# Weight residuals on VectorE alone, and the short chunk's value products in two column halves, in a fused attention, expert and MLP kernel

## The chip, the cores and the metric

The kernel runs on one core of a Trainium2 chip. The metric is the device time of one execution in microseconds (us), the median of several runs. A core has the engines TensorE (PE; its weight loads are shown apart as PEld), VectorE (DVE), ScalarE (ACT), GpSimd (POOL) and SyncE (SP), which issues most of the DMAs. Every engine works through its own instructions in order, and semaphores tie them together.

## The reference

Three parts run one after another. Each takes the output of the part ahead of it.

```python
# attention: 2 batches, 8 heads, 576 tokens, head size 64, with a position bias per head
scores = scale * q @ k.T + bias[h, i, j]
attn = exp(scores - max) / sum;  x = attn @ v              # -> 1152 tokens x 512
# experts: 8 of them, 512 -> 1024 -> 512, one expert per token, up to 288 tokens each
e = argmax(x @ w_gate);  y = gate * (relu(x @ w1[e]) @ w2[e])   # 0 for tokens over the capacity
# MLP: 512 -> 2048 -> 512
h = y @ w_in;  out = max(0.01 * h, h) @ w_out
```

## The kernel before, in words

**Attention.** The 576 query rows of a batch are four chunks of 128 rows and a short chunk of 64. `order` lists the ten (batch, chunk) pairs; each has four units, one per pair of heads, so there are 40 units, n = 0 to 39. The short chunks are units 16 to 19 (first batch) and 36 to 39 (second batch, the last of all). The loop at the end of the function is a software pipeline written out by hand. In turn n, PE makes the scores of unit n+1 (`s0`, `qk`, tile `St`, L329), transposes the weights of unit n (`tr`, tile `pt`, L362 to L368) and multiplies those of unit n-1 by V (`pv`, tile `xp`, L399 for full chunks, L402 and L404 for short ones). DVE adds the bias and takes the maximum (`ttr`, L341); ACT makes the exponential (`expo`, tile `A`, L352) and copies the transposed weights (L372). `prep`, `hooks`, `fin_a`, `fin_b` and `fin_c` hang routing, loads and clean-up on given turns. In a short chunk two heads share one unit: rows 0 to 63 of the score tile are head 2p, rows 64 to 127 are head 2p+1. `pv` of such a unit multiplies all 128 columns of V of both heads by all 128 rows and `fin_a` (L412) reads only the two 64x64 blocks on the diagonal.

**Residuals.** Matrices of the expert and MLP stages are used as a pair of float32r numbers, high part and residual, and each product is three matmuls (high times high, high times low, low times high; L856 to L858, L1191 to L1193). `wsplit` makes the pair for a weight tile of 128x1024: ACT casts it into `P[:, 0]` (L671), and an engine given by the caller writes the difference into `P[:, 1]` (L672).

**Experts.** `big_step` does one of eight steps of a block of up to 288 tokens: it splits the weights that are two steps ahead, then does two groups of the up (steps 0 to 3) or down product. The first block's first two splits stand in `hooks` at turns 36 and 37; the block itself follows the attention, then a second block (`big_last`) and a block of up to 64 tokens (`small`).

**MLP.** `chunk` takes 608 tokens through 16 weight tiles in the order `PO`: four up steps, four down steps, four up, four down. An up step has four half groups (`up_half`): PE multiplies 12 times into one of three PSUM tiles `g` (L856 to L858); ACT makes 0.01 times it (L880); DVE takes the maximum (L881, which frees the PSUM tile); a group later `split_h` makes the pair (ACT L888, DVE L889, tile `hq`). Between the groups `next(cv)` puts one of the three DVE operations (`conv_op`, L685, L687, L689) that turn the 64-bit weight words of `w_in` and `w_out` into floats, tile `raw`. Step i first calls `wsplit` for the tile of step i+2; in an up step that tile is the one whose third `conv_op` ran in the step before. The down steps (`down_tok`) use PE alone, besides `wsplit` and `conv_op`.

Of the kernel before, what the change touches and what calls it, by code (L numbers as in the profile page):

```python
# [26 lines left out]
NFULL = S // 128  # L27
# [47 lines left out]
def tile_attention_moe_mlp(ctx, tc, qc, kc, vc, wpk, cst, ctok, cap, wm, wo, out):  # L75
    nc = tc.nc
# [56 lines left out]
    def setup_late():  # L133
        nc.sync.dma_start(tok, ctok)
        nc.sync.dma_start(cpi, cap.to_broadcast([128, 2]))
        nc.gpsimd.memset(acc, 0.0)
        nc.gpsimd.memset(oh, 0.0)
        nc.gpsimd.memset(kcum, 0.0)
        nc.gpsimd.memset(pat, 0.0)
        nc.gpsimd.memset(pat[:, :, 0:1].bitcast(I32), OOB)  # L140
        nc.gpsimd.tensor_tensor(out=II, in0=ident[:, 0:CAPS], in1=ident[:, CAPS : 2 * CAPS], op=ALU.add)

        nc.gpsimd.memset(pre, 0.0)
        nc.gpsimd.memset(pre[:, DM : DM + 1].bitcast(I32), OOB)
# [3 lines left out]
    def prefill(t, a, n):  # L148
        w = t.shape[1]
        nc.sync.dma_start(t.rearrange("(a p) c -> p a c", p=128)[:, a : a + n], pre[:, 0:w].unsqueeze(1).to_broadcast([128, n, w]))  # L150
# [60 lines left out]
    def flush(n):  # L211
        g = drip.pop(n)
        while g in dq:
            run(dq.pop(0))

    def queue(n, g):
        drip[n] = g
        dq.append(g)
# [172 lines left out]
    def pv(c, p, ATs, Vs, xp):  # L391
        V, vt, vd = Vs
        AT, AX_ = ATs
        if c < NFULL:
            for t in range(NFULL + 1):
                for j in range(2):
                    h = 2 * p + j
                    w, a = (V[:, t, 64 * h : 64 * h + 64], AT[:, j, 128 * t : 128 * t + 128]) if t < NFULL else (vd[:, p, 64 * j : 64 * j + 64], AX_)
                    nc.tensor.matmul(xp[64 * j : 64 * j + 64, p, :], w, a, start=t == 0, stop=t == NFULL)  # L399
        else:  # L400
            for t in range(NFULL):
                nc.tensor.matmul(xp[:, p, :], V[:, t, 128 * p : 128 * p + 128], AT[:, 0, 128 * t : 128 * t + 128],  # L402
                                 start=t == 0, stop=False)
            nc.tensor.matmul(xp[:, p, :], vt[:, 128 * p : 128 * p + 128], AX_[0:64], start=False, stop=True)  # L404

    def fin_a(c, rs, xp, last):
        xt = rt.tile([128, NP, 128], F32, name="xt", tag="xt", bufs=1)
# [256 lines left out]
    raws, Ps, xhls, regs = [], [], [], {}  # L664
# [5 lines left out]
    def wsplit(raw, P_, eng):  # L670
        nc.scalar.copy(P_[:, 0], raw)  # L671
        eng.tensor_tensor(out=P_[:, 1], in0=raw, in1=P_[:, 0].bitcast(F32), op=ALU.subtract)  # L672
# [87 lines left out]
    def hooks(n):  # L760
        if n == 1:
            setup_late()
        if n == 12:
            nc.vector.tensor_copy(capf, cpi[:, 0:1])
        if n in PF:
            prefill(srt, 3 * PF.index(n), 3)
        if n == 16:
            nc.sync.dma_start(sid.rearrange("(p a) c -> p a c", p=128), pat)
        if n == NB0 + 4:
            queue("acc0", route_acc(0, range(NCH)))  # L770
        if n == NB0 + 5:
            flush("acc0")
            queue("route0", route0())
            queue("first0", first0())
        if n == SC[0]:
            flush("route0")
        if n in SC:
            scatter(0, SC.index(n))
        if n in ACC1:
            queue("acc1", route_acc(1, [i for i in range(NFULL) if ACCN[i] == n]))  # L780
        if n - 1 in ACC1:
            flush("acc1")
        if n == RF + 1:
            flush("first0")
            regs["e0"] = nc.values_load(ints[0:1, 2:3], engines=[SP], min_val=0, max_val=E_N - 1)
            regs["x0"] = nc.values_load(ints[0:1, 3:4], engines=[SP], min_val=0, max_val=S)
        if n in (CV0 - 3, CV0 - 2, CV0 - 1):
            g_w64(n - CV0 + 3)
        k, odd = divmod(n - CV0 - 2, 2)
        if odd == 0 and 0 <= k < len(CVA):  # L790
            nc.sync.dma_start(wsc[CVA[k]], cvd[k])
            if k + 3 < len(CVA):
                g_w64(k + 3)
        if n == 36:
            for t, m in xtiles:
                if t % 2 == 0:
                    kr = p1.tile([128, 2, S], F32, name="x0r", tag="kr", bufs=KRB)
                x0.append(kr[:, t % 2, 0:DM])
                nc.sync.dma_start(x0[t][0:m], srt[sl_(regs["x0"] + 128 * t, m), 0:DM])
            copy_id(regs["x0"], 0, CAPB)  # L800
        if n in (33, 34, 36, 37):
            raws.append(wp.tile([128, 1024], F32, name="raw", tag="bs", bufs=5))
            wdma(wsrc(regs["e0"], len(raws) - 1), raws[-1])
        if n in (36, 37):
            Ps.append(wp.tile([128, 2, 1024], F32R, name="P", tag="G", bufs=3))
            wsplit(raws[n - 36], Ps[-1], nc.gpsimd)
        if n == 38:
            xhls.append(wp.tile([128, 2, NP, CAPB], F32R, name="xhl0", tag="G", bufs=3))
        if n in (38, 39):
            wdma(wsrc(regs["e0"], n - 34), raws[n - 38])  # L810
        if n >= 38:
            x_tr(n - 38, x0[n - 38], xhls[0])
        if n == N:
            route1a()
            scatter(1, 0)
            scatter(1, 1)

    def tail_part(fa):
        att.close()
        mo = ctx.enter_context(tc.tile_pool(name="mo", bufs=1))  # L820
        spare = wp.tile([128, 1024], F32, name="spare", tag="bs", bufs=5)
# [226 lines left out]
        def big_step(j, base, eng, post=None, prep=False, last=None):  # L1048
            split((j + 2) % 8, eng, R0 if post else R8)
            if j == 7:  # L1050
                down_last(Ps[3], F1 // 128, CAPB, lambda m: (yout(base, m), last and last(m)))
            for mm in range(2):
                if j < 4:
                    up_group(Ps[j], j, mm, xhls[0], CAPB)
                elif j < 7:
                    down_group(Ps[j - 4], j - 4, mm, F1 // 128, CAPB)
                if post:
                    post(j, mm)
            if prep and j >= 5:
                prep_x(j - 5)  # L1060

        def big_last():
            xbase, base = bval(0, 1, 1, [SP]), bval(0, 1, 2, [ACT, DVE, SP])
            copy_id(xbase, base, CAPB)
            ne = bval(1, 0, 0, [SP])
            for j in range(8):
                big_step(j, base, nc.gpsimd)
                if j > 2:
                    wdma(wsrc(ne, j - 3), R8[j - 3])

# [133 lines left out]
        def chunk(c, first):  # L1204
            w = MCS[c]
            groups = [(t, min(128, w - 128 * t)) for t in range(-(-w // 128))]
            cv = convs()
            PP = [Ds[i] if first and i < 2 else Ps[i % 4] for i in range(16)]
            if not first:
                for i in range(3):  # L1210
                    wdma(wsc[i], raws[i])
                yprep(c)
            for i in range(3, 5):
                conv_start(i)
            if not first:
                for i in range(2):
                    wsplit(raws[i], PP[i], nc.vector)
            for i in range(13):
                if i + 2 < 16:
                    wsplit(spare if first and i == 0 else raws[(i + 2) % 4], PP[i + 2], nc.gpsimd)  # L1220
                q = PO[i]
                if q < 8:
                    for g in (0, 2, 1, 3):
                        up_half(PP[i], 2 * q + g // 2, w // 2 * (g % 2), w // 2)
                        if g != 3:
                            next(cv, None)
                else:
                    for kk in range(2):
                        for t, n in groups:
                            down_tok(PP[i], 2 * (q - 8) + kk, t, n)  # L1230
                            if t == 0:
                                split_h()
                            if 2 * t + kk in DCV:
                                next(cv, None)
                if i == 5:
                    for t, n in groups:
                        nc.sync.dma_start(idg[0:n, t], sid[MOF[c] + 128 * t : MOF[c] + 128 * t + n].bitcast(I32))
            wsplit(raws[15 % 4], PP[15], nc.vector)
            for t, n in groups:
                for i in range(13, 16):  # L1240
                    for kk in range(2):
                        down_tok(PP[i], 2 * (PO[i] - 8) + kk, t, n)
                emit(t, n)
# [21 lines left out]
    for n in range(N + 1):  # L1265
# [9 lines left out]
        if n + 1 < N:  # L1275
            b, c, p = units[n + 1]
# [12 lines left out]
        if n >= 1:  # L1289
            b, c, p = units[n - 1]  # L1290
# [74 lines left out]
```

## Time and profile before

| | |
|---|---|
| median of 3 runs | 407.12 us (406.49 to 407.96) |
| the profiled execution | 408.05 us, of which its span, first to last instruction, is 406.3 us |
| busy, share of the span | PE 93%, PEld 77%, DVE 76%, ACT 60%, POOL 34% |
| granted TensorE clock, mean | 0.986 of full speed |
| DMA | 81.79 MB, mean 201 GB/s |

Matmuls overlap in the pipeline, so a busy PE need not be one at its peak; where PE lost time shows in the distance from start to start. A row of the timeline gives the start, the duration and, in brackets, the idle time before it and what ended that.

### The profile page before, as it was taken

Reading aid. Unit: us, or ns where it says so; the run is one execution under the profiler, and the core shown is the slowest. Engines: PE = TensorE matmul, PEld = TensorE weight load, DVE = VectorE, ACT = ScalarE, POOL = GpSimd, SP = SyncE. Lnnn points to the kernel's source line nnn. Section 1 sums busy time; section 2 is a strip of 40 time slices with the busy share of each in tenths; the row PEclk is TensorE's granted clock in tenths of the full one; section 3 lists DMA queues with packets and bytes.
Section 4 is the critical chain, followed back from the end, with each engine's and each line's share of the span. In section 5 each row is a group of like instructions: output and inputs, shape, how many; then the busy total and the mean of one; then the engine's idle time right before and its main releaser. Section 6 shows DMA issues by size and latency. Waiting matters only on the chain. (4 is left out here: it accounts for less than half of the span.)

```text
span 406.3 us, 8427 instructions
## 1 busy us (share of the span) xinstructions
PE 375.9 (93%) x2990; PEld 312.6 (77%) x2990; DVE 307.7 (76%) x733; ACT 242.9 (60%) x522; POOL 139.1 (34%) x110
## 2 busy tenths in 40 slices
PE   4777999988999999999999999999999999899993
PEld 2234666756688888988889999998988778788872
DVE  5998989899854888899458972137899999999310
ACT  3857898788865878767654875556544222455100
POOL 1445857574101110212332206840242255222311
PEclk9999899999999999999998999999999999999997
DMA  7979599798879938889185299683243366530011
GB/s 180 320 235 322 157 330 313 274 297 250 216 236 262 353 135 233 224 253 250 46 236 201 69 327 343 217 289 114 106 173 127 106 207 206 209 106 2 19 59 51
DMA packets 34050, 81.79 MB, mean 201 GB/s; under 512 B 8427, under 2 KB 8811, under 8 KB 31952
## 3 DMA queue, kind: packets, MB, share of 16 engines
q1 hardware_dynamic: 32880, 78.70, 61.3%
q0 software_dynamic: 1120, 2.48, 1.7%
q8 instruction: 25, 0.41, 0.4%
q14 instruction: 25, 0.20, 0.2%
HBM read 59.11 MB, written 23.20 MB: 203 GB/s over the span
## 5 line engine op out<-in xcount | busy, mean ns | idle before, releaser
L341 DVE CUSTOM_DVE_ANT_0 sv<-St,bt 128x576 f32<-128x576 f32 x72 | 52.9, 750 | 30.8 <-PE St L329 18.8
L672 POOL TENSOR_TENSOR P<-raw,P 128x1024 fp32r<-128x1024 f32 x18 | 45.3, 2521 | 76.6 <-ACT P L671 63.5
L352 ACT ACTIVATE A<-sv,mx 128x576 f32<-128x576 f32 x72 | 59.3, 837 | 3.2 <-DVE mx L341 3.0
L329 PE MATMUL St<-K,Q 128*128 128x320 f32 (+1 forms) x320 | 53.6, 310 | 2.6 <-DVE mx L341 2.2
L329 PEld LDWEIGHTS St<-K,Q 128*128 128x128 f32 x320 | 43.9, 189 | 14.6 <-issue 8.4
L182 PE MATMUL pb<-Gt,WP 128*32 128x272 f32 (+17 forms) x352 | 42.1, 505 | 13.3 <-DVE Gt L165 7.5
L269 POOL TENSOR_TENSOR Q<-qr,Q 128x256 fp32r<-128x256 f32 x22 | 16.9, 769 | 99.9 <-ACT Q L261 62.1
L165 DVE TENSOR_SCALAR Gt<-WL,bp 128x400 f32<-128x400 f32 (+17 forms) x98 | 49.4, 563 | 0.1
L671 ACT CAST P<-raw 128x1024 fp32r<-128x1024 f32 x27 | 28.3, 1048 | 28.3 <-DVE raw L689 22.7
L362 PE MATMUL pt<-CS,A 128*128 128x128 f32 x288 | 41.5, 284 | 1.3 <-ACT A L352 0.8
L372 ACT COPY AT<-pt 128x512 f32<-128x512 f32 x40 | 23.3, 583 | 29.2 <-PE pt L362 28.9
L362 PEld LDWEIGHTS pt<-CS,A 128*128 128x128 f32 x288 | 38.1, 206 | 2.2 <-ACT A L352 1.3
L169 POOL TENSOR_SCALAR Gt<-WL,bp 128x528 f32<-128x528 f32 (+12 forms) x17 | 34.1, 2009 | 8.2 <-DVE Gt L165 7.3
L399 PE MATMUL xp<-AT,V 128*64 128x128 f32 x512 | 35.9, 284 | 0.0
L399 PEld LDWEIGHTS xp<-AT,V 128*64 128x64 f32 x512 | 28.0, 139 | 9.8 <-issue 9.5
L182 PEld LDWEIGHTS pb<-Gt,WP 128*32 128x32 f32 x352 | 12.4, 110 | 29.8 <-DVE Gt L165 14.7
L856 PE MATMUL g<-yhl,P 128*128 128x304 f32 x96 | 30.5, 318 | 3.9 <-DVE gfa L881 3.9
L193 ACT ACTIVATE bs<-pb,CS 128x288 f32<-128x288 f32 (+53 forms) x60 | 27.2, 500 | 10.1 <-PE pb L182 9.5
L1193 PE MATMUL ac<-P,hq 128*128 128x512 f32 (+1 forms) x80 | 31.5, 394 | 0.0
L1191 PE MATMUL ac<-P,hq 128*128 128x512 f32 (+1 forms) x80 | 31.5, 394 | 0.0
L1192 PE MATMUL ac<-P,hq 128*128 128x512 f32 (+1 forms) x80 | 31.5, 394 | 0.0
L889 DVE TENSOR_TENSOR hq<-gfa,hq 128x304 fp32r<-128x304 f32 x32 | 28.9, 902 | 1.4 <-ACT hq L888 1.4
(322 smaller groups left out, 907.4 us busy)
## 6 DMA issues: line engine op xcount, KB each, us to landing
bt<-scr SPq DMA_DIRECT2D x24, 576.0 KB, 6.0
w<-wo SPq DMA_DIRECT2D x13, 1024.0 KB, 5.0
scr<-bs SPq DMA_DIRECT2D x36, 295.5 KB, 4.2
raw<-wm SPq DMA_DIRECT2D x14, 512.0 KB, 6.2
w<-wm SPq DMA_DIRECT2D x10, 512.0 KB, 5.7
srt<-pre SPq DMA_DIRECT2D x6, 771.0 KB, 8.4
qr<-qc SPq DMA_DIRECT2D x16, 256.0 KB, 5.7
w64g<-wo SPq DMA_DIRECT2D x3, 1024.0 KB, 10.3
```

The costliest lines, as they stand in the source:

```text
L165: nc.vector.tensor_scalar(G, src, bp[:, g : g + 1], 0.0, op0=ALU.add, op1=ALU.max)
L169: nc.gpsimd.tensor_scalar(G, src, bp[:, g : g + 1], 0.0, op0=ALU.add, op1=ALU.max)
L182: nc.tensor.matmul(pb[32 * q : 32 * q + 32, 0 : hi - lo], W2, gs[:, q, lo:hi], start=True, stop=True)
L329: nc.tensor.matmul(St[:, o + lo : o + hi], Q[:, h - 2 * p, w, :], K[:, h - 2 * p, lo:hi], start=n == 0, stop=n == len(seq) - 1)
L341: nc.vector.tensor_tensor_reduce(out=sv, in0=St, in1=bt[:, jb], scale=-0.125, scalar=3.0e38, op0=ALU.add, op1=ALU.min, accum_out=mx)
L352: nc.scalar.activation(A[:, :, j], sv, AF.Exp, bias=mx, scale=-1.0, accum_out=rs[:, col : col + 1])
L362: nc.tensor.transpose(pt[:, 128 * t : 128 * t + 128], A[:, 128 * t : 128 * t + 128, j], ident)
L399: nc.tensor.matmul(xp[64 * j : 64 * j + 64, p, :], w, a, start=t == 0, stop=t == NFULL)
L672: eng.tensor_tensor(out=P_[:, 1], in0=raw, in1=P_[:, 0].bitcast(F32), op=ALU.subtract)
L1191: nc.tensor.matmul(ps, hh, wh, start=k == 0, stop=False)
L1192: nc.tensor.matmul(ps, hh, wl, start=False, stop=False)
L1193: nc.tensor.matmul(ps, hl, wh, start=False, stop=k == F2 // 128 - 1)
```

## The change

Three calls that gave `nc.gpsimd` to a weight split give `nc.vector`: the two in `hooks`, the eight of `big_last`, and the 13 in the loop of `chunk`. The loop `any_block`, which doesn't run with these inputs, keeps GpSimd. In `pv`, a short unit's five matmuls (128 columns of V by 128 rows) become ten, each head's 64 columns by its own 64 rows; the two halves of the output sit in different column halves of PE's array, as they do in full chunks.

```diff
@@ pv
-            for t in range(NFULL):
-                nc.tensor.matmul(xp[:, p, :], V[:, t, 128 * p : 128 * p + 128], AT[:, 0, 128 * t : 128 * t + 128],
-                                 start=t == 0, stop=False)
-            nc.tensor.matmul(xp[:, p, :], vt[:, 128 * p : 128 * p + 128], AX_[0:64], start=False, stop=True)
+            for t in range(NFULL + 1):
+                for j in range(2):
+                    r = slice(64 * j, 64 * j + 64)
+                    h = slice(128 * p + 64 * j, 128 * p + 64 * j + 64)
+                    w, a = (V[:, t, h], AT[:, 0, 128 * t + 64 * j : 128 * t + 64 * j + 64]) if t < NFULL else (vt[:, h], AX_[0:64, r])
+                    nc.tensor.matmul(xp[r, p, r], w, a, start=t == 0, stop=t == NFULL)
@@ hooks
-            wsplit(raws[n - 36], Ps[-1], nc.gpsimd)
+            wsplit(raws[n - 36], Ps[-1], nc.vector)
@@ big_last
-                big_step(j, base, nc.gpsimd)
+                big_step(j, base, nc.vector)
@@ chunk
-                    wsplit(spare if first and i == 0 else raws[(i + 2) % 4], PP[i + 2], nc.gpsimd)
+                    wsplit(spare if first and i == 0 else raws[(i + 2) % 4], PP[i + 2], nc.vector)
```

Line numbers behind `pv` are two higher in the changed kernel. In its order of instructions, DVE around the `hooks` of turns 36 and 37 (L341 is `ttr`, of units 38 and 39 here; the row with `mx` alone reads its minimum out) had before:

```order
L415 TENSOR_SCALAR rs<-rs 128x8
L341 ISA sv,mx<-St,bt 128x576
L341 ISA mx 128x1
L417 RECIPROCAL rec<-rs 128x8
L439 TENSOR_TENSOR xn<-px,rec 128x512
L341 ISA sv,mx<-St,bt 128x576
L341 ISA mx 128x1
```

and has now, with L674 the residual:

```order
L417 TENSOR_SCALAR rs<-rs 128x8
L674 TENSOR_TENSOR P<-raw,P 128x1024
L341 ISA sv,mx<-St,bt 128x576
L341 ISA mx 128x1
L419 RECIPROCAL rec<-rs 128x8
L441 TENSOR_TENSOR xn<-px,rec 128x512
L674 TENSOR_TENSOR P<-raw,P 128x1024
L341 ISA sv,mx<-St,bt 128x576
```

A residual stands ahead of each of the two `ttr`, so these wait behind it.

In the MLP, DVE around the end of one up step and the start of the next (`gfa` is the half group's float result) had before:

```order
L689 SCALAR_TENSOR_TENSOR raw<-w_3172,raw 128x1024
L881 TENSOR_TENSOR gfa<-g_3189,gfa 128x304
L889 TENSOR_TENSOR hq_3175<-gfa,hq_3173 128x304
L881 TENSOR_TENSOR gfa<-g_3190,gfa 128x304
L889 TENSOR_TENSOR hq_3175<-gfa,hq_3173 128x304
L685 TENSOR_SCALAR raw<-w_3171 128x1024
```

and has now:

```order
L691 SCALAR_TENSOR_TENSOR raw<-w_3212,raw 128x1024
L883 TENSOR_TENSOR gfa<-g_3229,gfa 128x304
L891 TENSOR_TENSOR hq_3215<-gfa,hq_3213 128x304
L674 TENSOR_TENSOR P_3210<-raw,P_3210 128x1024
L883 TENSOR_TENSOR gfa<-g_3230,gfa 128x304
L891 TENSOR_TENSOR hq_3215<-gfa,hq_3213 128x304
L687 TENSOR_SCALAR raw<-w_3211 128x1024
```

The residual came in ahead of the new step's first L881 (now L883); nothing else moved.

On PE, a short unit's products (turn 37) stood before between the transposes and those of the routed rows, `pxs`:

```order
L362 MATMUL pt<-CS,A 128x128 x4
L368 MATMUL pt_3049<-CS,A 64x128
L402 MATMUL xp<-AT,V 128x128 x4
L404 MATMUL xp<-AX__3001,vt 128x128
L723 MATMUL pxs<-CS,x0r 128x128 x4
```

and stand there now as:

```order
L362 MATMUL pt<-CS,A 128x128 x4
L368 MATMUL pt_3074<-CS,A 64x128
L406 MATMUL xp<-AT,V 64x64 x8
L406 MATMUL xp<-AX__3021,vt 64x64 x2
L725 MATMUL pxs<-CS,x0r 128x128 x4
```

Twice as many matmuls of a quarter of the output each; their place is the same.

## Rows read from the trace of the kernel before

**Rows 1.** Timeline of PE (start us, us): a stall, and where the second up stage begins and ends.
```profile
306.18 0.41 PE L856 MATMUL g<-yhl,P 128*128 128x304 f32 x1 [0.94 <-DVE gfa L881]
...
341.20 0.30 PE L856 MATMUL g<-yhl,P 128*128 128x304 f32 x1
...
346.08 0.30 PE L858 MATMUL g<-yhl,P 128*128 128x304 f32 x1
...
371.65 0.39 PE L1191 MATMUL ac<-P,hq 128*128 128x512 f32 x1
```

**Rows 2.** Timeline of DVE, third and fourth up step: start us, us, engine, line.
```profile
303.08 2.06 DVE L889 TENSOR_TENSOR hq<-gfa,hq 128x304 fp32r<-128x304 f32 x1
...
306.05 0.46 DVE L889 TENSOR_TENSOR hq<-gfa,hq 128x304 fp32r<-128x304 f32 x1
...
308.33 1.21 DVE L689 SCALAR_TENSOR_TENSOR raw<-w,raw 128x1024 uint32<-128x1024 uint32 x1
...
311.04 0.47 DVE L881 TENSOR_TENSOR gfa<-g,gfa 128x304 f32<-128x304 f32 x1 [0.73 <-ACT gfa L880]
```

**Rows 3.** Timeline of POOL, an up step and a down step.
```profile
302.41 2.40 POOL L672 TENSOR_TENSOR P<-raw,P 128x1024 fp32r<-128x1024 f32 x1 [5.95 <-ACT P L671]
...
326.19 2.91 POOL L672 TENSOR_TENSOR P<-raw,P 128x1024 fp32r<-128x1024 f32 x1 [4.68 <-ACT P L671]
```

**Rows 4.** Timeline of ACT, the cast ahead of the fourth up step's residual.
```profile
309.63 1.05 ACT L671 CAST P<-raw 128x1024 fp32r<-128x1024 f32 x1 [1.13 <-DVE raw L689]
```

**Rows 5.** Timeline of DVE, down steps and the second up stage's first L881.
```profile
326.87 3.31 DVE L689 SCALAR_TENSOR_TENSOR raw<-w,raw 128x1024 uint32<-128x1024 uint32 x1
...
346.41 0.47 DVE L881 TENSOR_TENSOR gfa<-g,gfa 128x304 f32<-128x304 f32 x1
```

**Rows 6.** Groups by line, DVE: x, busy us, mean ns of one, idle before.
```profile
L672 DVE TENSOR_TENSOR P<-raw,P 128x1024 fp32r<-128x1024 f32 x9 | 10.9, 1219 | 3.0 <-ACT P L671 1.8 <-DMA out<-pre 1.2
```

**Rows 7.** Page, part 6: DMA issues, KB each, median us to landing.
```profile
w<-wo SPq DMA_DIRECT2D x13, 1024.0 KB, 5.0
```

**Rows 8.** Timeline of PE, turn 37: products of a short unit (x: passes).
```profile
202.02 0.43 PE L444 MATMUL pl<-xt,WP 128*32 128x128 f32 x8
202.38 1.16 PE L402 MATMUL xp<-AT,V 128*128 128x128 f32 x8
203.47 0.48 PE L404 MATMUL xp<-AX__2949,vt 64*128 64x128 f32 x2
203.88 1.34 PE L329 MATMUL St<-K,Q 128*128 128x320 f32 x8
```

**Rows 9.** Timeline of PE: products of a full unit, two column halves.
```profile
198.50 1.09 PE L399 MATMUL xp<-AT,V 128*64 128x128 f32 x16
...
199.74 1.34 PE L329 MATMUL St<-K,Q 128*128 128x320 f32 x8
```

**Rows 10.** Timeline of PE: the same operation as L444 above, 64 columns wide.
```profile
214.08 0.33 PE L444 MATMUL pl<-xt,WP 128*32 128x64 f32 x8
214.33 0.61 PE L856 MATMUL g<-xhl,P 128*128 128x288 f32 x1
```

**Rows 11.** Timeline of ACT, turns 36 to 38.
```profile
200.73 1.05 ACT L671 CAST P<-raw 128x1024 fp32r<-128x1024 f32 x1
...
206.42 0.82 ACT L352 ACTIVATE A<-sv,mx 128x576 f32<-128x576 f32 x1
```

**Rows 12.** Timeline of DVE: `ttr` of unit 38.
```profile
201.11 0.76 DVE L341 CUSTOM_DVE_ANT_0 sv<-St,bt 128x576 f32<-128x576 f32 x1 [1.99 <-PE St L329]
```

**Rows 13.** Timeline of PE, turns 38 and 39; L453 is `fin_c`'s.
```profile
205.05 0.63 PE L362 MATMUL pt<-CS,A 128*128 128x128 f32 x4
...
207.53 0.64 PE L362 MATMUL pt<-CS,A 128*128 128x128 f32 x4
...
209.51 0.33 PE L453 MATMUL pl<-CS,lt 128*128 128x128 f32 x1
```

**Rows 14.** Windows: us, busy of PE, PEld, DVE, ACT, POOL, PEclk, DMA share, GB/s.
```profile
214.40:217.40 3.00, 3.00 (x14) 2.93 (x14) 2.81 (x13) 1.26 (x2) 1.02 (x1) 0.50 0.92 352
```

## The prediction

> **What bounds the kernel now.** I read the windows first, then PE's starts in the timeline, then the other engines around PE's gaps. By starts, PE is packed through both short chunks; the exceptions that matter are the MLP's up stages and the end of the attention.
>
> In an up step PE stalls about 1 us for L881, which frees a PSUM tile [rows 1]. The second up stage runs from 341.20 to 371.65, 30.45 us. Its matmuls start (346.08 - 341.20) / 35 = 0.139 us apart where nothing stalls, so its 4 x 48 need 26.8 us: 3.65 us are lost there. DVE sets this pace, and what stretches DVE is to be seen by laying two timelines over each other. One L889 of a step takes 2.06 us, the others 0.46 [rows 2]. The long one began at 303.08, in the middle of POOL's residual, 302.41 to 304.81 [rows 3], and ended 0.33 after it: it ran when POOL was done. L881, which reads PSUM, isn't held: the one at 311.04 took 0.47 [rows 2], though its step's residual had begun when the cast ended at 310.68 [rows 4]. In the down steps L689 is held in this way: 3.31 us from 326.87, over a residual from 326.19 to 329.10 [rows 3, 5], against 1.21 [rows 2]. So DVE's high busy share is partly waiting for POOL.
>
> **Up steps, removed and added.** Gone: 2.06 - 0.46 = 1.60 us of DVE for a held L889. Added: the residual on DVE, 1.22 us [rows 6], of which 0.08 overlap the next operation, so 1.14. But in order it must wait for ACT's cast, and the cast for the third conversion, L689. From the start of that L689: 1.21 to its end [rows 2], 0.09 to the cast (308.33 + 1.21 = 309.54; 309.63), 1.05 for the cast [rows 4], 0.06 handover, 1.14: the next step's first L881 starts 3.55 us after L689. Now it starts 2.71 after (308.33 to 311.04), so 0.84 are added there. A cycle thus changes by +0.84 - 1.60 = -0.76 us, from 8.35 (311.04 less 302.69, since L881 starts 0.39 ahead of the L889 at 303.08) to 7.6. PE's own need is 48 x 0.139 = 6.7, so PE still waits and the gain passes through. The first up stage has two such full cycles between its stalls: **-1.5**.
>
> **Down steps.** PE isn't waiting here, but DVE falls behind: the second up stage's first L881 runs at 346.41 [rows 5], though PE began the stage at 341.20 and its first group was ready for L881 some 2.4 us later (12 x 0.139, then 0.3 of pipeline and an ACT operation of 0.42). Four L689 are held by 2.1 each, 8.4 together; four residuals of 1.14 cost 4.6. DVE gets there 3.8 us sooner against PE, at 342.6 in the old time, before PE has the group. In the four up steps DVE then needs 4 x (8 x 0.39 + 0.61 + 3 x 1.14) = 28.6 us, plus up to 0.4 per cast, against PE's 26.8; but PE may run three PSUM tiles ahead, 3 x 1.67 us, which covers the difference. I take back 3.5 of the 3.65: **-3.5**. From 371.65 on PE runs without a wait, so what is gained there reaches the end.
>
> What can spoil it: the conversions read 1 MB of words per tile, 5.0 us from issue to landing [rows 7], asked for when the conversion two tiles back is done. Two cycles of 3.1 us of conversion plus a residual are a little more than that; if loads landed 1.5 us later, DVE would stand in order with everything behind it, and I would take 1.7 less, about half of the second stage's loss. Bounds of the two MLP terms together: -3.3 (so) to -6.9 (all that PE loses there: 3.65, and 2 x (8.35 - 6.7) in the first stage).
>
> **`big_last`.** Eight residuals of 1.14 go to DVE, in a stage where PE packs its matmuls and DVE has one operation of some 0.46 per group and is otherwise idle. They stand behind ACT's cast, but ACT, in order, was already held by that cast. Cover: PE's 1.6 us per group with two spare PSUM tiles. Taken at 0; without that cover it would be 8 x 1.14 = 9.1 us.
>
> **Short chunks, PE.** A short unit took 203.88 - 202.38 = 1.50 us: eight passes in 1.09 (a float32 matmul is two passes), two with 64 rows in 0.41, and about 0.2 in each of these parts is the change of form [rows 8]. The nearest row of the new form is a full unit, 20 passes in column halves, which took 1.24 us with 128 moving columns [rows 9], so the halves run side by side. What 64 moving columns are worth: L444, two steps of four tiles side by side, took 202.38 - 202.02 = 0.36 with 128 columns [rows 8] and 214.33 - 214.08 = 0.25 with 64 [rows 10], 0.055 less per step. Ten steps: 1.24 - 0.55 = 0.69, plus 0.15 for the change to 64 rows and 0.1 for a form change at the entry that most units didn't have: 0.95. Saving 0.45 (1.50 or 1.40 before, by the entry). Bounds: 0 (narrow columns save nothing: 1.24 + 0.25) to 0.55.
>
> Here the Trainium skill speaks against it: TensorEngine Tiling (Array Packing), Instruction Overhead, gives each matmul about 60 cycles of overhead and advises not to take the tiling from a dimension that is already small. If that overhead came on top of each step, 64 columns would cost (60 + 64) / (60 + 128) = 0.66 of 128, an estimate by which a unit saved about 0.25, the first chunk 1.0, and the sum below were 0.6 smaller. L444's rows fell by nearly the whole half of the columns, 0.055 of the 0.11 that a pass of 128 takes in the L402 row ((1.09 - 0.2) / 8), so I go by the rows.
>
> First short chunk, units 16 to 19: PE is packed before and after it, up to unit 36, and DVE waits for PE there. 4 x 0.45 = 1.8, of which I keep **-1.6** for places where DVE or ACT will now be late.
>
> **Second short chunk: the wait that the change adds.** The two residuals of `hooks` stand ahead of `ttr` of units 38 and 39. The cast runs from 200.73 to 201.78 [rows 11], the residual from 201.84; `ttr` of unit 38 moves from 201.11 [rows 12] to 202.98, its exponential ends near 204.65, and its transposes come at 205.05 - 0.4: no stall yet [rows 13]. The second cast stands on ACT behind that exponential and a short copy: 204.75 to 205.8. Residual to 207.0, `ttr` of unit 39 to 207.76, its exponential (0.82, started at 206.42 before [rows 11]) to 208.66. PE wants unit 39's transposes at 207.53 - 2 x 0.45 = 206.65 and gets them at 208.7: it stalls 2 us, and L453 comes at 208.7 + (209.51 - 207.53) - 0.45 = 210.25 instead of 209.51 [rows 13]. Behind L453 hangs the routing chain on DVE, which sets when the first expert block starts. So here the saving is eaten: **+0.7**.
>
> **Sum.** -1.5 - 3.5 + 0 - 1.6 + 0.7 = -5.9 us. The profiled execution took 408.05 and would take 402.15; it lay 0.93 above the median, so for the median 407.12 - 5.9 = **401.2**.
>
> **Rivals.**
> - *The clock falls once more.* PE ran at a granted 0.50, its 1.2 GHz level, from 214.4 to 217.4 [rows 14], right after the thin stretch behind L453. The new stall of 2 us makes a second thin stretch. Another 3 us at half clock costs up to 1.5 where PE is the bound, but part would lie over the routing chain: 402.4 to 402.7.
> - *Column halves save nothing* (bounded by passes or loads): first chunk 0, second +1.2 (stall until 208.7, without savings behind it): 407.12 - 5.0 + 1.2 = 403.3.
> - *The conversions' loads hold DVE* and only half of the second stage's loss comes back: 407.12 - 5.9 + 1.7 = 402.9.
> - *Slower: the long L889 and L689 have another cause than POOL.* Then DVE, with no slack in the up steps, gets 1.14 more per step: 8 x 1.14 = 9.1 in place of -5.0, less 0.9 of the attention: 415. It decides from the point where a held operation shrinks by less than the 0.84 that a cycle gains. Against it: the long operations end with POOL's residual each time, and L881 at the same moment isn't long.
> - *No change* would need the up stages' gain to be eaten by all of the others together.
>
> **How the numbers follow.** Forecast as summed 0.52; clock 0.16; halves worthless 0.10; loads 0.14; slower 0.05; no change 0.03. Runs of this kernel differ by some 0.3%, 1.2 us, which I use as what can be told from no change. The first four cases are faster: 0.92; same 0.03; slower 0.05. The range reaches from the low bounds (-6.9 for the MLP, -1.8 for the first chunk, 0 for the second: 398.4, of which I take 398.5) to the rivals on the faster side with two of them together: 404.5.
>
> **What would show it.** Right: no L889 above 0.5 us, no L689 above 1.3; PE's cycle in the first up stage near 7.6 us; the second stage near 27 us; a short unit's products near 0.95 us; a stall of about 2 us ahead of unit 39's transposes. Wrong: long DVE operations that stay, DVE waiting for `w` loads in the MLP, a stretch at half clock before L453, or short units that still take 1.4 us.

## The result and the profile after

The changed kernel's median is 404.51 us over 6 runs (402.68 to 409.04), against 407.88 (406.49 to 408.99) for the kernel before. The ratio is 0.9912, 95% interval 0.9885 to 0.994; the run of 409.04, like one of 408.67 when the same kernel was run again, lies in a slower state and is left out of the ratios. The change is faster, by 3.4 us where 5.9 were forecast; the median of all six lies 0.01 us above the range, that of the other five, 404.32, inside it. The profiled execution is the fastest of the six: 402.68 us, 5.4 less than the profiled one of before. So the trace and the median tell different things, and the experiments had to say why.

The first row is the page's list of engines. DVE's busy share rose from 76% to 78% although it took over 23 residuals. The two windows under it are the up stages (columns as in [rows 14]).

```profile
PE 370.8 (92%) x3070; PEld 307.8 (77%) x3070; DVE 311.3 (78%) x756; ACT 242.6 (61%) x522; POOL 81.6 (20%) x87
```

```profile
282.82:311.77 28.95, 28.04 (x192) 27.01 (x193) 27.69 (x50) 17.90 (x40) 0.00 (x0) 1.00 0.45 164
339.49:366.29 26.80, 26.80 (x194) 26.80 (x193) 24.72 (x42) 14.29 (x32) 0.00 (x0) 1.00 0.32 115
```

The second up stage took 30.45 us before [rows 1]; now it takes 26.80 and PE is busy in all of it. The first still has stalls. DVE's timeline shows its cycle, from residual to residual (L674), and the start of the second up stage:

```profile
293.31 1.23 DVE L674 TENSOR_TENSOR P<-raw,P 128x1024 fp32r<-128x1024 f32 x1 [0.35 <-ACT P L673]
...
296.59 1.22 DVE L689 SCALAR_TENSOR_TENSOR raw<-w,raw 128x1024 uint32<-128x1024 uint32 x1
...
300.01 0.47 DVE L891 TENSOR_TENSOR hq<-gfa,hq 128x304 fp32r<-128x304 f32 x1
300.82 1.23 DVE L674 TENSOR_TENSOR P<-raw,P 128x1024 fp32r<-128x1024 f32 x1 [0.35 <-ACT P L673]
...
341.82 0.47 DVE L883 TENSOR_TENSOR gfa<-g,gfa 128x304 f32<-128x304 f32 x1 [1.59 <-ACT gfa L882]
```

A cycle takes 300.82 - 293.31 = 7.51 us (8.35 before). No L891 of these stages exceeds 0.47, where one took 2.06 [rows 2]. At 341.82 DVE waits for the stage's first group; before it came to it at 346.41 [rows 5].

PE's timeline: a short unit of the first chunk, then turns 37 to 39 of the second, which answer to [rows 8, 13].

```profile
129.25 0.69 PE L406 MATMUL xp<-AT,V 128*64 128x64 f32 x16
129.87 0.33 PE L406 MATMUL xp<-AX__1769,vt 64*64 64x64 f32 x4
130.13 1.07 PE L329 MATMUL St<-K,Q 128*128 128x320 f32 x6
...
202.70 1.33 PE L329 MATMUL St<-K,Q 128*128 128x320 f32 x8 [0.45 <-DVE mx L341]
...
207.72 0.74 PE L362 MATMUL pt<-CS,A 128*128 128x128 f32 x4 [1.64 <-ACT A L352]
...
209.37 0.33 PE L455 MATMUL pl<-CS,lt 128*128 128x128 f32 x1
...
212.22 0.41 PE L496 MATMUL prt<-acc,ones 128*128 128x40 f32 x2 [0.84 <-DVE acc L487]
```

A short unit's products now take 130.13 - 129.25 = 0.88 us. In the second chunk PE waits for unit 39's exponential. DVE's rows there show what that stands behind, two residuals, each ahead of a `ttr`:

```profile
200.74 1.23 DVE L674 TENSOR_TENSOR P<-raw,P 128x1024 fp32r<-128x1024 f32 x1 [2.69 <-ACT P L673]
201.88 0.75 DVE L341 CUSTOM_DVE_ANT_0 sv<-St,bt 128x576 f32<-128x576 f32 x1
...
204.78 1.22 DVE L674 TENSOR_TENSOR P<-raw,P 128x1024 fp32r<-128x1024 f32 x1 [1.23 <-ACT P L673]
205.92 0.75 DVE L341 CUSTOM_DVE_ANT_0 sv<-St,bt 128x576 f32<-128x576 f32 x1
```

Stage by stage, read from PE's starts in the two traces: the first short chunk kept 1.1 us, the second gave 0.9 back, the expert stages cost 0.3, the first up stage gained 1.8 and the second 3.65; together 5.4, the difference of the two spans (406.3 and 400.9).

### The profile page after: what moved, and what is told of

Its sections match the earlier page's. It is cut to its first block, busy times and chain, and to the rows that moved or that the text cites. A ratio compares the mean times of both kernels' runs of the same rounds, so it can differ in the third digit from the quotient of the medians.

```text
span 400.9 us, 8542 instructions
## 1 busy us (share of the span) xinstructions
PE 370.8 (92%) x3070; PEld 307.8 (77%) x3070; DVE 311.3 (78%) x756; ACT 242.6 (61%) x522; POOL 81.6 (20%) x87
## 5 line engine op out<-in xcount | busy, mean ns | idle before, releaser
L341 DVE CUSTOM_DVE_ANT_0 sv<-St,bt 128x576 f32<-128x576 f32 x72 | 52.8, 749 | 23.9 <-PE St L329 13.4
L352 ACT ACTIVATE A<-sv,mx 128x576 f32<-128x576 f32 x72 | 59.3, 838 | 8.7 <-DVE mx L341 6.9
L182 PE MATMUL pb<-Gt,WP 128*32 128x272 f32 (+17 forms) x352 | 43.5, 496 | 12.0 <-DVE Gt L165 9.3
L165 DVE TENSOR_SCALAR Gt<-WL,bp 128x400 f32<-128x400 f32 (+17 forms) x98 | 50.4, 574 | 0.1
L674 DVE TENSOR_TENSOR P<-raw,P 128x1024 fp32r<-128x1024 f32 x27 | 33.0, 1223 | 14.8 <-ACT P L673 12.7
L1203 POOL DMA_INDIRECT out<-osb,idg x5 | 4.8, 965 | 160.8 <-ACT osb L1202 154.3
L399 PE MATMUL xp<-AT,V 128*64 128x128 f32 x512 | 35.0, 279 | 0.0
L858 PE MATMUL g<-yhl,P 128*128 128x304 f32 x96 | 29.4, 306 | 0.8 <-DVE gfa L883 0.8
```

What stands on the lines that cost most here:

```text
L165: nc.vector.tensor_scalar(G, src, bp[:, g : g + 1], 0.0, op0=ALU.add, op1=ALU.max)
L182: nc.tensor.matmul(pb[32 * q : 32 * q + 32, 0 : hi - lo], W2, gs[:, q, lo:hi], start=True, stop=True)
L341: nc.vector.tensor_tensor_reduce(out=sv, in0=St, in1=bt[:, jb], scale=-0.125, scalar=3.0e38, op0=ALU.add, op1=ALU.min, accum_out=mx)
L352: nc.scalar.activation(A[:, :, j], sv, AF.Exp, bias=mx, scale=-1.0, accum_out=rs[:, col : col + 1])
```

## The experiments

Ratios are to the kernel before, in the same comparison.

**The 13 MLP residuals alone on DVE** (everything else as before).

```diff
-                    wsplit(spare if first and i == 0 else raws[(i + 2) % 4], PP[i + 2], nc.gpsimd)
+                    wsplit(spare if first and i == 0 else raws[(i + 2) % 4], PP[i + 2], nc.vector)
```

> Only the 13 residuals of the MLP on VectorE. Theory: the two up stages lose their stalls, 1.6 + 3.6 us: ratio 0.987, second up stage 26.8 us, cycle of the first 7.5 us; the attention and its clock as before. Rival, DVE's full queue costs what GpSimd's hold did: ratio 0.995 or more.

Measured: 0.9873 (0.9838 to 0.9907), 402.91 us. The window of the second up stage:

```profile
339.56:366.35 26.79, 26.79 (x193) 26.79 (x192) 24.88 (x42) 14.30 (x32) 0.00 (x0) 1.00 0.33 115
```

This one edit brings all that the whole change brings in the median. What the other edits do together is therefore nothing or a loss, as far as two ratios with overlapping intervals can tell.

**An idle GpSimd operation beside each of these residuals**: the change, and in each of the 13 steps a subtraction of a residual's size on GpSimd that nobody reads.

```diff
                     wsplit(spare if first and i == 0 else raws[(i + 2) % 4], PP[i + 2], nc.vector)
+                    nc.gpsimd.tensor_tensor(out=hy, in0=PP[i + 2][:, 0].bitcast(F32), in1=PP[i + 2][:, 0].bitcast(F32), op=ALU.subtract)
```

> The change, and in each of the 13 MLP steps GpSimd also does an operation of the residual's size (128x1024, two SBUF inputs) into a tile that nobody reads and nobody waits for. Theory, GpSimd's operations hold DVE's SBUF ones: DVE's own residual, which starts at the same cast, is held by nearly the whole 2.4 us, the cycle of an up step grows from 7.5 to about 9.6 and the up stages become longer than before: 8 to 14 us slower than the change, slower than before. Rival, the long L889 and L689 had another cause: within 0.5 us of the change.

Measured: 1.0206 (1.0173 to 1.0238), 415.86 us, some 11.4 above the change. Timelines of POOL and DVE, then the window of the second up stage:

```profile
357.23 2.87 POOL L1223 TENSOR_TENSOR hy<-P 128x1024 f32<-128x1024 f32 x1 [9.80 <-ACT P L673]
```

```profile
357.12 1.22 DVE L674 TENSOR_TENSOR P<-raw,P 128x1024 fp32r<-128x1024 f32 x1
358.26 0.47 DVE L883 TENSOR_TENSOR gfa<-g,gfa 128x304 f32<-128x304 f32 x1
358.64 1.78 DVE L891 TENSOR_TENSOR hq<-gfa,hq 128x304 fp32r<-128x304 f32 x1
```

```profile
342.73:377.40 34.67, 29.69 (x193) 28.98 (x192) 34.53 (x45) 14.72 (x32) 11.30 (x5) 0.90 0.38 130
```

Nothing waits for this operation, and yet L891 takes 1.78 us and ends at 360.42, 0.32 after POOL's at 360.10, the same 0.33 as in [rows 2, 3]. L883, which reads PSUM, runs in between in 0.47. The holding by GpSimd is shown, and the slower rival (another cause) is excluded. Two parts came out otherwise than expected. DVE's own residual isn't held: it starts 0.11 us ahead of GpSimd's operation and takes 1.22, and the L891 behind it pays. So a cycle of the first up stage grows to 8.83 us and not to 9.6. And of the second up stage's 34.67 us a part is clock: the trace has a granted 0.50 from 349.8 to 356.8. The Trainium skill, SBUF — State Buffer, SBUF: two separate sides, says that the two engines share a pair of ports under an exclusive lock, and that a DVE operation with two SBUF inputs, against a GpSimd operation that reads SBUF, blocks for the whole instruction when the other engine was first. The rows of POOL and L891 agree.

**`big_last`'s residuals back on GpSimd.** One word of the change is undone, `big_step(j, base, nc.gpsimd)`.

> The change with the eight residuals of big_last back on GpSimd. Theory (they are hidden in that stage, as the prediction took it): the stage from the first expert matmul to the MLP's first matmul keeps its length, 68.6 us in the change's trace, within 0.4, and the second up stage stays at 26.8; by the sum the time is the change's, 402.7 in its profiled run, within 1.2. Rival (GpSimd's residuals held DVE's operations there too, or DVE's residuals cost something there): the stage changes by more than 1 us. One look, so the stage's length decides and not the time.

Measured in a single execution: 404.48 us. Windows of the stage, and of a stretch at its beginning:

```profile
215.23:283.87 68.64, 67.18 (x497) 65.55 (x494) 38.28 (x99) 41.42 (x66) 24.24 (x14) 0.97 0.63 217
209.40:219.60 10.20, 10.20 (x65) 8.80 (x66) 8.01 (x37) 3.53 (x9) 0.99 (x1) 0.50 0.54 198
```

The stage has the same 68.6 us. The time missed by 1.8, though, and the second row points to the reason: 10.2 us on end at a granted 0.50, in a place where this kernel does just what the change does. The change's own trace has a half clock, as such a stretch at 0.50 is called from here on, from 214.3 to 217.7 only.

**The attention's parts apart.** Four kernels: the column halves alone; the change with the two residuals of `hooks` on GpSimd; this one with whole products in the second batch's short chunk; and that one with the hooks' residuals on DVE.

```diff
@@ hooks
-            wsplit(raws[n - 36], Ps[-1], nc.vector)
+            wsplit(raws[n - 36], Ps[-1], nc.gpsimd)
@@ pv
+        elif Vs is not Vt[0]:
+            for t in range(NFULL):
+                nc.tensor.matmul(xp[:, p, :], V[:, t, 128 * p : 128 * p + 128], AT[:, 0, 128 * t : 128 * t + 128],
+                                 start=t == 0, stop=False)
+            nc.tensor.matmul(xp[:, p, :], vt[:, 128 * p : 128 * p + 128], AX_[0:64], start=False, stop=True)
```

The halves alone:

> The column halves alone; all residuals stay on GpSimd. Theory: the first short chunk brings about 1.1 us by its end, as in the trace of the change; without the two residuals ahead of ttr the second short chunk keeps a part of its own 1.8 us, about 1.0: some 2 us less than before, ratio 0.995, and no PE stall of 2 us ahead of unit 39's transposes. The MLP's stages as long as before (30.7 and 30.45 us). Rival, the halves bring nothing in the end: ratio 1.000 within 0.001.

Measured: 0.9983 (0.9962 to 1.0004). The profiled execution gained 1.6 us, the median of ten runs 0.5. The interval leaves out the theory's 0.995 and reaches the rival's 0.999 to 1.001. The trace has no half clock between 203 and 220 us, although PE pauses for 0.84 us ahead of the routing's first matmul, where the kernel before pauses for 0.41.

The change with the hooks' residuals on GpSimd:

> The change with only the two residuals of turns 36 and 37 back on GpSimd. Theory: the stall of 1.6 us ahead of unit 39's transposes goes, the second short chunk gains about 1 us in place of losing 0.9, and with the stall goes the extra time at half clock that most runs of the change show (clock 0.972 to 0.988 against 0.993 in its profile): 1.9 us faster than the change's profile and 3 us faster than its median, ratio to before 0.982. Rival, the low clock comes from the narrow products: the ratio stays near 0.988 and the clock below 0.98 in most runs.

Measured: 0.9882 (0.9851 to 0.9912), the rival's figure, but not its clocks: they are 0.982 to 0.989, and it asked for less than 0.98. PE's timeline and the windows:

```profile
206.73 0.74 PE L362 MATMUL pt<-CS,A 128*128 128x128 f32 x4
...
211.24 0.41 PE L496 MATMUL prt<-acc,ones 128*128 128x40 f32 x2 [0.84 <-DVE acc L487]
```

```profile
212.10:218.50 6.40, 6.28 (x33) 5.59 (x34) 5.01 (x22) 1.67 (x3) 1.02 (x1) 0.50 0.72 277
```

The wait ahead of unit 39's transposes has gone, and the median has hardly moved. PE now ran 6.4 us at half clock, and the stage from the first expert matmul to the MLP took 69.83 us in place of 68.63; in it PE also waits 1.02 us for rows from memory, of which more below. My first theory, that the wait alone ate the attention's gain, falls.

With whole products in the second batch's short chunk:

> Column halves in the first batch's short chunk only; the second batch's short chunk has whole products as before; the hooks' residuals on GpSimd, the other residuals on DVE. Theory (the second chunk's halves bring nothing once the wait behind them sets the end, the first chunk's bring about 1.1 us that stay): 0.987 of the 13 MLP residuals alone, less 1.1 us, so a ratio of 0.983 to 0.985. Rival (the halves of either chunk are paid back by a lower granted clock): 0.987 to 0.989, as with the MLP residuals alone or with all halves, at granted clocks of 0.98 in most runs in place of 0.99.

Measured: 0.983 (0.9804 to 0.9855), 401.36 us, at clocks of 0.983 to 0.996; the theory's figure. It is the version to keep: it beats both kernels. Its interval overlaps those of the change and of the kernel ahead of it by 0.0015 at most, or not at all, so that it is faster is likelier than by how much. PE's row of unit 39's transposes and the stage's windows:

```profile
206.35 0.40 PE L362 MATMUL pt<-CS,A 128*128 128x128 f32 x2
```

```profile
213.16:280.55 67.39, 65.55 (x499) 63.72 (x493) 48.04 (x110) 41.46 (x66) 5.54 (x6) 1.00 0.65 222
213.40:216.40 3.00, 3.00 (x24) 2.98 (x24) 2.81 (x13) 1.56 (x3) 1.02 (x1) 1.00 0.93 366
```

Whole products, hooks' residuals on DVE:

> The change with whole products in the second batch's short chunk: column halves in the first batch's only, all residuals on DVE, the hooks' too. Theory (the hooks' residuals on DVE make unit 39 wait, with or without halves): unit 39's transposes come near 207.7 in place of 206.35 as with these residuals on GpSimd, and the ratio is 0.983 plus 1.2 us: 0.986, or up to 0.990 where the clock falls behind the wait. Rival (without the halves the wait disappears in PE's longer products): 0.982 to 0.984.

Measured: 0.9885 (0.9859 to 0.991). PE's timeline and a window:

```profile
208.27 0.74 PE L362 MATMUL pt<-CS,A 128*128 128x128 f32 x4 [1.09 <-ACT A L352]
```

```profile
215.20:218.50 3.30, 3.30 (x19) 3.23 (x16) 3.08 (x13) 1.53 (x3) 0.99 (x1) 0.54 0.94 379
```

Counted from the start of unit 38's scores (199.23 here, 198.56 with these residuals on GpSimd), the transposes come 1.25 us later (9.04 against 7.79), and a half clock follows that the other trace doesn't have. So there is a two by two:

| second short chunk | whole products | column halves |
|---|---|---|
| hooks' residuals on GpSimd | 0.983 | 0.9882 |
| hooks' residuals on DVE | 0.9885 | 0.9912 and 0.9892 (the change, twice) |

Either edit costs about 2 us in the median. One delays unit 39's transposes by 1.25 us; the other delays nothing and only lengthens the pause ahead of the routing's first matmul, from 0.42 us to 0.84.

**The change once more.**

> The changed kernel once more, for the spread of its runs and a second trace. Theory (what the median lost against the sum is the granted clock, not a wait): its runs lie between 402.5 and 405.5, those at a clock of 0.97 to 0.98 above 404 and those near 0.99 below 403; in the trace the two up stages keep their lengths within 0.3 us (second 26.8) and what differs from the first trace lies in stretches at a granted clock of 0.50. Rival: a wait differs between runs (a load that lands late, a DVE operation), and a stage differs without a half clock in it.

Measured: 0.9892 (0.984 to 0.9944), from 402.39 us at a clock of 0.988 to 406.3 at 0.985: a wider spread than expected, which the mean clock alone doesn't order. Windows of this trace:

```profile
206.70:208.20 1.50, 0.00 (x0) 0.00 (x0) 0.83 (x4) 0.88 (x3) 0.00 (x0) 1.00 1.07 385
208.60:211.60 3.00, 3.00 (x28) 2.38 (x27) 1.00 (x4) 0.82 (x3) 0.00 (x0) 0.50 0.70 280
215.70:218.30 2.60, 2.60 (x18) 2.05 (x17) 2.34 (x15) 1.26 (x2) 0.50 (x1) 0.50 0.96 370
287.50:290.20 2.70, 2.70 (x13) 2.70 (x12) 2.50 (x5) 1.98 (x4) 0.00 (x0) 0.50 0.84 352
343.03:369.83 26.80, 26.80 (x194) 26.80 (x192) 24.75 (x42) 14.30 (x32) 0.00 (x0) 1.00 0.32 115
```

The first row is the wait for unit 39, in which PE does nothing. Right behind it, the rest of the second chunk runs at the 1.2 GHz level; the first trace had 1.00 there. This trace ends 3.5 us later than the first: 0.55 were there before the wait, 1.8 come between the wait and the first expert matmul, 0.6 in the experts, 0.5 in the first up stage, which has a half clock of its own. The second up stage is the same to 0.01 us. The 1.8 and the 0.5 lie in stretches at half clock, as the theory has it. The 0.6 in the experts don't: there the rival holds, a wait that differs. The second block multiplies rows that GpSimd's DMAs have put into the table `srt` (L565) and that SP loads from it as `xr`. PE waits 1.69 us for them in this trace and waited 0.38 in the first. Rows of PE, POOL and DVE in this trace, then of PE and POOL in the first:

```profile
242.99 1.41 PE L725 MATMUL g<-CS,xr 128*128 128x128 f32 x8 [1.69 <-DMA xr<-srt]
226.94 1.94 POOL L565 DMA_INDIRECT srt<-xn,sl  x1 [2.99 <-DMA srt<-xn,sl]
226.80 1.21 DVE L674 TENSOR_TENSOR P<-raw,P 128x1024 fp32r<-128x1024 f32 x1
```

```profile
239.99 1.45 PE L725 MATMUL g<-CS,xr 128*128 128x128 f32 x8 [0.38 <-DMA xr<-srt]
226.77 0.97 POOL L565 DMA_INDIRECT srt<-xn,sl  x1 [1.60 <-DMA srt<-xn,sl]
```

GpSimd's issue of such a DMA took 1.94 us here where it began in the middle of a residual on DVE, and 0.97 in the first trace where none ran. In the 14 traces of this document 70 such issues stand behind the attention. The 15 that began during a residual on DVE, and more than 0.2 us before its end, took 1.23 to 1.94 us and ended 0.78 to 0.87 after it; the other 55 took 0.91 to 1.02. The residuals of the first block were on DVE in the kernel before too; what differs is whether the two meet. No run tests this by itself.

**Work that nobody reads, to keep PE busy.** Matmuls of `ones` by `ident`, 128 columns each, into free or later overwritten PSUM columns: three ahead of the routing's first matmul, one ahead of the `pr` matmul, and for the change itself six more ahead of unit 39's transposes (`fill` is 6 there and 0 elsewhere).

```diff
@@ ranks
+        for _ in range(3 if b and n == NFULL else 0):
+            nc.tensor.matmul(pr[:, 128:256], ones, ident, start=True, stop=True)
@@ fin_b
+            if b:
+                nc.tensor.matmul(pr[:, 128:256], ones, ident, start=True, stop=True)
@@ tr
+            for _ in range(fill):
+                nc.tensor.matmul(pt[:, 0:128], ones, ident, start=True, stop=True)
```

The change, hooks' residuals on GpSimd, four such matmuls:

> The kernel with the hooks' residuals on GpSimd, and four additional matmuls of 128 columns on TensorE whose results nobody reads, in the thin stretch between the attention's last products and the first expert block. Theory (the idle stretch of PE there is what the half clock behind it follows from): the half clock at 212 to 219 us is shortened or gone, the stage from the first expert matmul to the MLP falls from 69.8 to about 67, the ratio to the kernel before is 0.981 to 0.984. Rival (the clock was lowered by something earlier, the narrower products of the attention among them): half clock stays at that place, the ratio stays at 0.988 as without the additional matmuls.

Measured: 0.9806 (0.978 to 0.9833), 400.78 us; without them 0.9882. No half clock is left between 203 and 220 us. The stage did not shorten as expected, to 67, but took 69.1, for PE now waits 1.87 us for the second block's rows (three of GpSimd's issues took 1.73 to 1.87 us there):

```profile
238.53 0.66 PE L729 MATMUL g<-CS,xr 128*128 128x128 f32 x4 [1.87 <-DMA xr<-srt]
```

The change as it is, ten such matmuls:

> The change as it is (both residuals of the hooks on DVE), with ten additional matmuls whose results nobody reads: six in the wait ahead of unit 39's transposes, three ahead of the routing's first matmul, one ahead of the pr matmul. The wait itself stays. Theory (the median lost against the sum because PE's granted clock falls behind that wait and behind the routing's thin stretch): no half clock between 203 and 220 us in the trace, and the ratio is that of the kernel with the hooks on GpSimd and four such matmuls, 0.981, plus 1.4 us of wait: 0.983 to 0.986. Rival (the wait costs its own time, and the clock has nothing to do with the stretch): 0.989 to 0.991, as the change without them.

Measured: 0.9865 (0.9847 to 0.9883), 402.88 us. PE's timeline, then windows:

```profile
205.93 1.50 PE L362 MATMUL pt<-CS,ones 128*128 128x128 f32 x12
207.74 0.74 PE L364 MATMUL pt<-CS,A 128*128 128x128 f32 x4 [0.30 <-ACT A L352]
```

```profile
207.00:211.00 4.00, 3.70 (x55) 2.90 (x54) 2.06 (x10) 2.19 (x7) 0.00 (x0) 1.00 0.66 256
214.40:217.40 3.00, 3.00 (x24) 2.98 (x24) 2.81 (x13) 1.55 (x3) 0.99 (x1) 1.00 0.86 329
```

Unit 39 still comes at 207.7: the wait stays, and PE is busy in it. The whole stretch is at 1.00, and the interval leaves out the rival's 0.989 to 0.991, although its upper end is above the theory's 0.986. Against the 0.9892 of the second comparison, whose interval is wide, the gain is likely and not shown.

Halves in the first batch's short chunk only, hooks on GpSimd, four such matmuls:

> Halves in the first batch's short chunk only, hooks' residuals on GpSimd, and the four additional matmuls of the thin stretch ahead of the first expert block (results nobody reads). Theory (the half clock behind this stretch comes in some runs and the additional work keeps it away): ratio 0.979 to 0.982, and the runs' clocks at 0.99. Rival (without the second chunk's halves the clock doesn't fall there, and the additional matmuls cost their own 0.3 to 0.5 us or nothing): 0.983 to 0.984.

Measured: 0.9862 (0.9844 to 0.9881), no better than without them. The figure is above both expectations. Its trace has no half clock there either, but PE waits for the second block's rows:

```profile
238.89 0.66 PE L734 MATMUL g<-CS,xr 128*128 128x128 f32 x4 [1.03 <-DMA xr<-srt]
240.24 0.66 PE L734 MATMUL g<-CS,xr 128*128 128x128 f32 x4 [0.70 <-DMA xr<-srt]
```

Without the additional matmuls it waited 0.59 us in all, and the stage from the first expert matmul to the MLP took 67.39 us in place of 68.57. Three of GpSimd's issues took 1.58 to 1.85 us here and 0.91 to 0.98 there.

The kernel before, with the four matmuls:

> The kernel before, none of the change in it, with the four additional matmuls (results nobody reads) of the thin stretch ahead of the first expert block. It tells how much of what such matmuls gave the variants of the change was to be had before the change too. Theory (the kernel before loses one half clock of some 3 us there, worth 1.0 to 1.2 us, and the change's variants lose a second one): no half clock between 203 and 220 us, and a ratio of 0.996 to 0.998. Rival (the kernel before loses as much to the clock there as the change does): 0.990 to 0.993. Third, the clock costs the kernel before nothing there, since the experts wait for something else: 0.999 to 1.001.

Measured: 0.9992 (0.9979 to 1.0005) over 12 runs, the third case. Its trace has 1.00 where [rows 14] have 0.50:

```profile
214.00:217.40 3.40, 3.40 (x32) 2.95 (x32) 3.03 (x20) 1.53 (x3) 0.42 (x1) 1.00 0.82 312
```

So such matmuls are worth nothing in the kernel before. With the second chunk's halves they go with a lower median (0.9806 against 0.9882, 0.9865 against 0.9912 and 0.9892), without them they don't (0.9862 against 0.983).

## Why the prediction was right, and where not

- **Bound, and the MLP terms** (-1.5 and -3.5): right. The trace shows -1.8 and -3.65, the cycle 7.51 us (7.6 forecast). One reading was loose: the held L689 of [rows 5] ended 1.08 us after POOL's residual and not with it, which is nearly its own 1.21, so it too ran when POOL was done. The experiment with the MLP residuals alone gives 0.9873, 1.27% of 408 or 5.2 us, where the two terms are 5.0.
- **The loads' rival**: DVE did wait for `w` in four down steps, 1.3 us in all, where nobody waited for DVE. It cost nothing.
- **`big_last` at 0**: right, the stage is 68.6 us either way.
- **A short unit** at 0.95 us: measured 0.88. The estimate from the Trainium skill (TensorEngine Tiling (Array Packing), Instruction Overhead) of 0.25 saved is too small: 1.40 to 1.50 became 0.88. **First chunk** -1.6: -1.5 at unit 21, of which 1.1 stay from unit 22 on. The experiment with the first chunk's halves against the MLP residuals alone is 0.983 against 0.9873, 1.8 us, a difference between ratios of two comparisons, in which `big_last`'s residuals differ too.
- **Second chunk, the wait**: right as a mechanism. In the time of before, unit 39's transposes were forecast at 208.7; they come at 207.72, which is 208.8 with the 1.1 us that the first chunk gained. The scores' wait of 0.45 at 202.70 wasn't forecast.
- **Second chunk, the size: this is the step that failed.** The term of +0.7 counted only the wait, and the trace of the fastest run agrees with it (+0.9). In the median the two edits of this chunk cost 2.5 us or more (0.9892 and 0.9912 against 0.983). The rival of the clock named the place and a cause, but was given 0.16 and priced as one half clock of 3 us at up to 1.5 us. Measured, in the second trace: 1.8 us behind the wait, with a half clock in it. Another 0.6 us in the experts are the wait for the second block's rows, which no term of the sum has. And the loss isn't bound to the wait: the halves with the hooks' residuals on GpSimd, which only make PE finish earlier, cost as much.

Ahead of the first expert block PE is not the bound; the rows there end its waits with ACT (L352) and DVE (`acc`). There time saved on PE turns into idle time, and the PE clock can then fall for the matmuls behind. In the first block this costs PE 0.5 to 2 us: up to the second block's rows it needs, waits left out, 24.1 to 24.3 us in the six traces without a half clock there and 24.7 to 26.1 in the eight with one. But in 11 of the 14 traces PE then waits 0.25 us or more for those rows, so that not all of it reaches the end. Shown are the half clocks, their places and that none is left there with the additional matmuls (no half clock between 203 and 220 us in any of the four traces with such matmuls, and one in eight of the ten without them, the kernel before among these). Not shown is that the clock alone makes the loss in the median, for a trace shows one execution. Open is what decides it in a single run: the kernel of 0.983 paused ahead of the routing's first matmul as long as the kernel before (0.42 and 0.41 us) and shows no half clock behind it, and the kernel with the halves alone paused for 0.84 without one. Open too is why the additional matmuls help with the second chunk's halves (0.9806) and not without (0.9862); one trace of the latter points to the second block's rows, which came 1.2 us later. Between comparisons the same kernel differs by 0.002 in its ratio, so that no ranking within 0.003 is meant here.

## What to carry to other kernels

Before an operation goes to GpSimd because it has time, look at what DVE does meanwhile: an operation that is off every path can still hold DVE, and two timelines laid over each other show it by their common end. A saving on PE counts only where PE is the bound; where it waits for others anyway the saving becomes idle time, and the granted clock of the stretch behind has to be read as well, and the next wait for memory too, which may take what the clock gives back. One profile of the fastest run doesn't show that: compare the granted clocks of all runs, and the traces of two.

## What the runs showed of the hardware

The half clock also comes without unit 39's wait: 6.4 us at 0.50 behind the routing stretch in which PE had paused for 0.84 us ahead of 211.24, and 10.2 us in another trace. In the former the first block's matmuls start 0.24 us apart at 0.50 (214.27, 214.51) and 0.13 apart at 1.00 (219.10, 219.23). The Trainium skill, TensorE: Matmul & The Clock Gate, HAM oscillation, describes a matmul kernel in which each wait for a load, longer than the waits here, makes the clock fall again. The rows of the second trace, 1.5 us idle and then 0.50, look like it; those of the first, which stand here, show 1.5 us idle and then 1.00, so it needn't come.

```profile
206.20:207.70 1.50, 0.00 (x0) 0.00 (x0) 0.78 (x4) 0.93 (x3) 0.00 (x0) 1.00 1.04 415
208.60:211.70 3.10, 2.78 (x49) 2.23 (x49) 2.20 (x14) 1.71 (x6) 0.00 (x0) 1.00 0.37 144
```
